# Packing the first chunk's attention scores into 15 steps, three of them shared by two pairs of head groups, and building the constant mask tile later

## The chip, the cores and the metric

The kernel runs on one core of a Trainium2 chip. The metric is the device time of one execution in microseconds (us). Of the kernel before, three timed runs gave 310.59, 310.47 and 310.94 us; their median is 310.59 us.

## What is computed

A transformer block on 2048 rows of 640 numbers: a layer norm, then sliding-window causal attention (32 heads of 20, each row sees itself and the 255 rows before it) and a gated unit, both on the normed input, both added to the input.

```python
xn = _layernorm(x)
qkv = (xn @ wqkv)                    # q, k, v: 32 heads of 20
scores = q @ k.T * 20 ** -0.5
mask = (i - j >= 0) & (i - j < 256)  # i: row of q, j: row of k
p = softmax(where(mask, scores, -1e9))
attn = (p @ v) @ wo
h = sigmoid(xn @ w_gate) * (xn @ w_up)
out = x + attn + h @ w_down
```

## The kernel before, in words

The 2048 rows are worked in four chunks (c = 0 to 3) of 512. Inside a chunk, the unit of attention is 64 rows (U = 64): a chunk has 8 units of queries, and its keys are its own 8 units and, from chunk 1 on, the last 4 of the chunk before. The 32 heads are 8 groups of 4; two groups form a **pair** (o = 0, 2, 4, 6), one on the upper and one on the lower 64 partitions of a score tile.

A **step** is one score tile: `scores` (L484) fills a 4-bank PSUM tile `ps` with up to 8 columns of units for each of 4 heads, ScalarE takes the exponential of it into a `pT` tile (L497), and masks follow. A step lists **pieces** (j, q, n, col): key unit j against n query units from q on, put at column col. A piece is 8 matmuls, 2 groups by 4 heads. A key unit meets at most 5 query units; the first of them needs the causal (diagonal) mask and the fifth the window's (old) mask. GpSimd makes these masks on `pT` by `affine_select` (L508), two instructions for a mask, one for each half of the partitions. In the last kind of step of the later chunks the two masks stand side by side, and VectorE does both by one minimum with a constant tile `edge` (L501). `edge` holds zeros and a huge number; `make_edge` (L239) builds it on GpSimd with one memset (L240) and four selects (L244).

In the first chunk no key lies before row 0, so a pair needs 30 columns of units. `FIRST` lays them out in 4 steps of 8, 8, 6 and 8, that is 16 steps for four pairs. A later chunk needs 5 steps a pair (`LATER`).

`pv` (L512) multiplies a pair's `pT` tiles by v into two PSUM accumulators `acc` (L524); `finish_group` and `scale_group` turn and divide the result on VectorE. `pv` takes the pieces in an order of its own: widest first, in rounds with narrow ones, four-wide ones last.

The order of the work is written by hand (manual schedule): each engine runs its instructions in the order in which the program issues them, and waits on semaphores. The main loop (from L723) goes through the list of all steps t. It issues a pair's `pv` when t is in `due`: in chunk 0 two steps after the pair's last step, in later chunks one. Then it issues the step's scores, and then **fill**: other matrix work (gate and up projections `gu`, the next chunk's q, k and v, the down and output projections `out`), pulled from a queue of generators in equal shares by cost (`credit`, `cuts`). A generator's unit is for instance five matmuls of 512 columns (`pg`, L415, or `pu`, L422). Normalising the next chunk is mixed into this fill (`g_norms`): VectorE statistics, `rstds` on GpSimd (L267, L268), `xn` on VectorE (L273).

Before the loop stand chunk 0's norm, v, q and k; `make_edge()` is called right behind `g_qk(0)`. GpSimd has nothing between its memsets at the start and the first step's masks, so its queue reaches `edge` at once.

Five `pT` tiles rotate. `ps` is a single tile.

Of the kernel before, what the change touches and what calls it, by code (L numbers as in the profile page):

```python
# [17 lines left out]
CW = 512  # L18
NCH = S // CW
SBC = CW // P  # L20
HG = 4
NG = H // HG
# [6 lines left out]
SCALE = DH ** -0.5  # L29
# [6 lines left out]
MIN = mybir.AluOpType.min  # L36
# [3 lines left out]
EXP = mybir.ActivationFunctionType.Exp  # L40
# [5 lines left out]
U = 64  # L46
# [13 lines left out]

FIRST = (
    dict(pieces=((0, 0, 5, 0), (5, 5, 3, 5)), diag=(0, 2), old=(4, 1), units=8),
    dict(pieces=((1, 1, 5, 0), (6, 6, 2, 5), (4, 7, 1, 7)), diag=(0, 2), old=(4, 1), units=8),
    dict(pieces=((2, 2, 5, 0), (7, 7, 1, 5)), diag=(0, 2), old=(4, 1), units=6),
    dict(pieces=((3, 3, 5, 0), (4, 4, 3, 5)), diag=(0, 2), old=(4, 1), units=8),
)
LATER = (
    dict(pieces=((2, 2, 5, 2), (-3, 0, 2, 0), (7, 7, 1, 7)), diag=(2, 2), old=(1, 2), units=8),  # L70
    dict(pieces=((3, 3, 5, 1), (6, 6, 2, 6), (-4, 0, 1, 0)), diag=(1, 2), old=(0, 2), units=8),
    dict(pieces=((0, 0, 5, 3), (-2, 0, 3, 0)), diag=(3, 1), old=(2, 2), units=8),
    dict(pieces=((1, 1, 5, 0), (5, 5, 3, 5)), diag=(0, 2), old=(4, 1), units=8),
    dict(pieces=((-1, 0, 4, 0), (4, 4, 4, 4)), late=3, units=8),
)
SPAN = 5


def steps_of(c):
    return [(o, step) for o in range(0, NG, 2) for step in (LATER if c else FIRST)]  # L80


def pieces_of(g):
# [10 lines left out]
def kernel(  # L94
# [11 lines left out]
    nc = tc.nc  # L106
# [4 lines left out]
    def pool(name, bufs, **kw):  # L111
        return ctx.enter_context(tc.tile_pool(name=name, bufs=bufs, **kw))
# [11 lines left out]
    op = pool("op", 7)  # L124
# [105 lines left out]
    for n in (6, 4):  # L230
        ps = ps_d.tile([P, CW], FP32, name="pwarm", tag="d")
# [179 lines left out]
    def g_gu(c, f0, f1):  # L411
        for f in range(f0, f1):
            pg = ps_d.tile([P, CW], FP32, name="pg", tag="d")
            for d in range(DC):
                nc.tensor.matmul(pg, lhsT=part(wg, d, f), rhs=xnT[c][:, d, :],  # L415
                                 start=(d == 0), stop=(d == DC - 1))
            th = tp.tile([P, CW], FP32, name="th")
            nc.scalar.activation(out=th, in_=pg, func=TANH, scale=0.5)  # L418
            yield 5 * MM
            pu = ps_d.tile([P, CW], FP32, name="pu", tag="d")  # L420
            for d in range(DC):
                nc.tensor.matmul(pu, lhsT=part(wu, d, f), rhs=xnT[c][:, d, :],  # L422
                                 start=(d == 0), stop=(d == DC - 1))
# [57 lines left out]
            yield 10 * 136  # L481


    def scores(c, o, step):  # L484
        pt = pp.tile([P, HG, PTW], BF16, name="pT")
        ps = ps_s.tile([P, HG, CW], FP32, name="ps")
        for j, q, n, col in step["pieces"]:
            kc, kb = divmod(c * CW // U + j, CW // U)
            for a in range(2):
                for i in range(HG):  # L490
                    nc.tensor.matmul(  # L491
                        ps[a * U:(a + 1) * U, i, col * U:(col + n) * U],
                        lhsT=qk["k", kc, o // GH][32 * i:32 * i + DH, o % GH + a, kb * U:(kb + 1) * U],
                        rhs=qk["q", c, o // GH][32 * i:32 * i + DH, o % GH + a, q * U:(q + n) * U],
                        start=True, stop=True)
        width = step["units"] * U
        nc.scalar.activation(out=pt[:, :, 0:width], in_=ps[:, :, 0:width], func=EXP, scale=SCALE)  # L497
        if "late" in step:
            u = step["late"]
            view = pt[:, :, u * U:(u + 2) * U]  # L500
            return pt, lambda: nc.vector.tensor_tensor(out=view, in0=view, in1=edge, op=MIN)  # L501

        for (u, n), base, sign in ((step["diag"], 0, 1), (step["old"], -1, -1)):
            for a in range(2):
                two = pt[a * U:(a + 1) * U].rearrange("p h (a b) -> p h a b", a=2)
                k, b = divmod(u, SPAN)
                view = two[:, :, k:k + n, b * U:(b + 1) * U]
                nc.gpsimd.affine_select(out=view, in_=view, pattern=[[0, HG], [0, n], [sign, U]],  # L508
                                        compare_op=GE, fill=0.0, base=base, channel_multiplier=-sign)
        return pt, None  # L510

    def pv(c, o, parts):  # L512
        accs = [ps_d.tile([P, CW], FP32, name="acc", tag="d") for _ in range(2)]

        flat = sorted(((pt, *piece) for step, pt in parts for piece in step["pieces"]), key=lambda x: -x[3])
        late = [x for x in flat if SPAN - 1 == x[3]]
        rounds = ([x for x in flat if x[3] == SPAN], [x for x in flat if x[3] < 3], [x for x in flat if x[3] == 3] + late)
        flat = [x for r in itertools.zip_longest(*rounds) for x in r if x]
        for k, (pt, j, q, n, col) in enumerate(flat):
            kb, u = divmod(c * CW // U + j, 2)  # L520
            for a, acc in enumerate(accs):
                for i in range(HG):
                    h = o // 2 * HG + i
                    nc.tensor.matmul(  # L524
                        acc[32 * i:32 * i + 32, q * U:(q + n) * U],
                        lhsT=vt[kb][a * U:(a + 1) * U, u, h * VW:h * VW + 32],
                        rhs=pt[a * U:(a + 1) * U, i, col * U:(col + n) * U],
                        start=(k == 0), stop=(k == len(flat) - 1), skip_group_check=True)
        for a, acc in enumerate(accs):
            finish_group(c, o + a, acc)  # L530
# [145 lines left out]
    for _ in g_qk(0):  # L676
        pass
    load_rest()
    make_edge()

    fill = Fill()
    GU = 10 * MM
# [3 lines left out]
    def later(load, *args):  # L686
        load(*args)
        yield 0
# [2 lines left out]
    norms2 = g_norms(2, True)  # L691
    norms3 = g_norms(3, False)
    fill.add("gu0a", mix(g_gu(0, 0, 4), norms1, 4, 1, False), 4 * GU)
    fill.add("gu0b", mix(g_gu(0, 4, 12), norms1, 0), 8 * GU)
    fill.add("x2", later(load_x, 2), 0)
    fill.add("wo_i", later(turn_wo), 0)
# [13 lines left out]
    fill.add("out2", g_out(2, (), g_gu(3, 0, 1)), OUT + GU)  # L710
    fill.add("gu3", g_gu(3, 1, 12), 11 * GU)

    todo = [(c, k, o, step) for c in range(NCH) for k, (o, step) in enumerate(steps_of(c))]
    ends = {(c, o): t for t, (c, _, o, _) in enumerate(todo)}
# [8 lines left out]
    for t, (c, k, o, step) in enumerate(todo):  # L723
# [11 lines left out]
        pt, late = scores(c, o, step)  # L735
        parts.setdefault((c, o), []).append((step, pt))
# [11 lines left out]
    c = NCH - 1  # L748
# [62 lines left out]
```

## Time and profile before

| | |
|---|---|
| median of three runs | 310.59 us (310.47 to 310.94) |
| the profiled execution's own time | 309.89 us |
| its span in the profile | 308.2 us |
| TensorE matmul busy | 300.2 us, 97% of the span |
| ScalarE, VectorE, GpSimd busy | 64%, 56%, 55% |
| exponentials, 128x2048 / 128x1536 | 1878 / 1446 ns each, 72 and 4 of them |
| score matmuls and pv matmuls | 1440 and 1440 |

How to read it: times are microseconds from the start of the span. In the timeline a line gives start, duration, engine, source line, operation, the tile written and those read, how many instructions were merged into the line, and in brackets how long the engine was idle before it and what released it. A merged line names only the form of its first instruction. PE is TensorE's matmul, DVE is VectorE, ACT is ScalarE, POOL is GpSimd. Matmuls overlap in the pipeline, so the duration of one is longer than the distance to the next start; the distances between starts are the cost. The 1.7 us between the span and the execution's own time lie outside of the program's instructions.

### The profile page before, as it was taken

To read this page: it belongs to the slowest core of one execution; us is meant where nothing else is said; L and a number is where in the kernel's file an instruction comes from. 1 tells how busy PE (TensorE), PEld (TensorE's weight loads), DVE (VectorE), ACT (ScalarE), POOL (GpSimd) and SP (SyncE) were. 2 spreads that over 40 slices of the span, in tenths; PEclk is the share of its full clock that TensorE was granted. 3 is DMA by queue.
4 is the path that set the end of the run, shared out by engine and by line. 5 is a ranking of instruction groups with operands and counts; after the bars stand their busy time and mean duration, and the time that the engine had idled before them with its cause. 6 is when DMAs were issued, how large, how long until landed. Compare 5 with 4: busy or idle time off the path is not lost.

```text
span 308.2 us, 9938 instructions
## 1 busy us (share of the span) xinstructions
PE 300.2 (97%) x4276; PEld 167.5 (54%) x4311; DVE 171.2 (56%) x339; ACT 198.4 (64%) x197; POOL 168.7 (55%) x308
## 2 busy tenths in 40 slices
PE   7999999999999999999999999999999999999995
PEld 3654444545657654554457664554546664444774
DVE  5633657648698364497946164383734536363523
ACT  6923777698854649888674647878585547687000
POOL 6000687687874828576682728557372937566000
PEclk9999999999999999999999999999999999999999
DMA  7997986984709253720015312660000200000202
GB/s 216 366 315 249 317 168 200 348 231 146 232 2 126 70 178 123 219 81 2 3 24 87 87 57 74 196 189 0 5 0 2 86 26 21 2 2 9 81 21 67
DMA packets 40461, 35.68 MB, mean 116 GB/s; under 512 B 10561, under 2 KB 39873, under 8 KB 40385
## 3 DMA queue, kind: packets, MB, share of 16 engines
q1 hardware_dynamic: 39552, 34.27, 38.4%
q8 instruction: 34, 0.56, 0.8%
q10 hardware_dynamic: 864, 0.77, 0.8%
q14 instruction: 11, 0.08, 0.1%
HBM read 23.63 MB, written 10.26 MB: 110 GB/s over the span
## 4 chain that ended last, share of the span: by engine, by line
PE 96%; issue 1%; DMA 1%; DVE 1%; ACT 0%; SPq 0%
PE y L436 18%; PE pu L422 17%; PE pg L415 17%; PE pqk L300 14%; PE ps L491 9%; PE pv L330 7%; PE y L443 7%; PE acc L524 6%; DMA xc<-in_A_x_dram 1%; PE pt L280 0%; ACT xn L621 0%; DVE xn L273 0%; DVE xn L632 0%; DVE stats L253 0%; SPq L157 0%
## 5 line engine op out<-in xcount | busy, mean ns | idle before, releaser
L508 POOL TENSOR_SCALAR_AFFINE_SELECT pT<-pT 64x512 bf16<-64x512 bf16 (+1 forms) x256 | 157.1, 614 | 109.3 <-ACT pT L497 97.0
L497 ACT ACTIVATE pT<-ps 128x2048 bf16<-128x2048 f32 (+1 forms) x76 | 141.0, 1855 | 59.8 <-PE ps L491 57.9
L426 DVE SCALAR_TENSOR_TENSOR h<-th,pu 128x512 bf16<-128x512 f32 x48 | 32.8, 683 | 51.4 <-PE pu L422 45.0
L422 PE MATMUL pu<-xnT,wu 128*128 128x512 bf16 x228 | 59.0, 380 | 0.7 <-issue 0.2
L415 PE MATMUL pg<-xnT,wg 128*128 128x512 bf16 x226 | 58.5, 380 | 1.0 <-issue 0.3
L436 PE MATMUL y<-wd,h 128*128 128x320 bf16 (+2 forms) x396 | 56.8, 295 | 0.0
L300 PE MATMUL pqk<-xnT,wqkv 128*128 128x512 bf16 x191 | 45.4, 381 | 0.6 <-issue 0.2
L436 PEld LDWEIGHTS <-h 128*128 128x128 bf16 x396 | 36.7, 98 | 15.9 <-issue 1.8
L418 ACT ACTIVATE th<-pg 128x512 f32<-128x512 f32 x48 | 28.6, 595 | 15.5 <-PE pg L415 15.4
L415 PEld LDWEIGHTS <-wg 128*128 128x128 bf16 x240 | 22.2, 98 | 25.8 <-issue 1.8
L422 PEld LDWEIGHTS <-wu 128*128 128x128 bf16 x240 | 22.0, 98 | 25.5 <-issue 2.0
L300 PEld LDWEIGHTS <-wqkv 128*128 128x128 bf16 x200 | 22.5, 119 | 18.9 <-issue 1.6
L536 DVE STREAM_TRANSPOSE t<-acc 128x512 f32<-128x512 f32 x32 | 21.1, 696 | 20.1 <-PE acc L524 20.1
L491 PE MATMUL ps<-qT,kT 20*64 20x320 bf16 (+4 forms) x1440 | 32.1, 260 | 0.0
L491 PEld LDWEIGHTS <-kT 20*64 20x64 bf16 x1440 | 15.4, 103 | 24.8 <-issue 21.4
L447 DVE SCALAR_TENSOR_TENSOR rows<-y,rows 128x320 bf16<-128x320 f32 x30 | 14.4, 487 | 25.9 <-PE y L443 25.8
L548 DVE TENSOR_TENSOR on<-t,rec 128x320 bf16<-128x320 f32 (+4 forms) x48 | 27.8, 579 | 1.1
L330 PE MATMUL pv<-wqkv,xnT 128*128 128x320 bf16 x160 | 26.0, 300 | 0.0
L443 PE MATMUL y<-wo,oc 128*128 128x320 bf16 (+2 forms) x165 | 24.2, 295 | 0.0
L339 DVE CAST v<-pv 64x320 bf16<-64x320 f32 x29 | 14.1, 487 | 12.6 <-PE pv L330 12.3
L524 PE MATMUL acc<-pT,v 64*32 64x320 bf16 (+4 forms) x1440 | 19.7, 253 | 0.0
L524 PEld LDWEIGHTS <-v 64*32 64x32 bf16 x1440 | 16.3, 91 | 5.7 <-ACT pT L497 1.7
(48 smaller groups left out, 156.7 us busy)
## 6 DMA issues: line engine op xcount, KB each, us to landing
qT<-sq SPq DMA_DIRECT2D x16, 256.0 KB
kT<-sk SPq DMA_DIRECT2D x16, 256.0 KB
sq<-st SPq DMA_DIRECT2D x20, 128.0 KB
sk<-st SPq DMA_DIRECT2D x20, 128.0 KB
out_dram<-rows SPq DMA_DIRECT2D x15, 160.0 KB
wg<-in_B_w_gate_dram SPq DMA_DIRECT2D x4, 480.0 KB
wu<-in_B_w_up_dram SPq DMA_DIRECT2D x4, 480.0 KB
xc<-in_A_x_dram SPq DMA_DIRECT2D x3, 640.0 KB
```

The source lines that it names most:

```text
L300: nc.tensor.matmul(ps, lhsT=wt[:, m, :], rhs=xnT[c][:, d, :], start=(d == 0), stop=(d == DC - 1))
L330: nc.tensor.matmul(ps[:, 0:HALF], lhsT=xnT[c][:, d, s * P:(s + 1) * P], rhs=wqkv[:, d, 2 * D + hf * HALF:2 * D + (hf + 1) * HALF], start=( ...
L415: nc.tensor.matmul(pg, lhsT=part(wg, d, f), rhs=xnT[c][:, d, :], start=(d == 0), stop=(d == DC - 1))
L418: nc.scalar.activation(out=th, in_=pg, func=TANH, scale=0.5)
L422: nc.tensor.matmul(pu, lhsT=part(wu, d, f), rhs=xnT[c][:, d, :], start=(d == 0), stop=(d == DC - 1))
L426: nc.vector.scalar_tensor_tensor(out=h, in0=th, scalar=1.0, in1=pu, op0=ADD, op1=MULT)
L436: nc.tensor.matmul(y[:, 0:cut[1] - cut[0]], lhsT=ht[c, f][:, s * P:(s + 1) * P], rhs=wd[:, f, cut[0]:cut[1]], start=(f == 0), stop=False)
L443: nc.tensor.matmul(y[:, 0:cut[1] - cut[0]], lhsT=oc[c, m][:, s * P:(s + 1) * P], rhs=wo[:, m, cut[0]:cut[1]], start=False, stop=(m == DC - 1))
L491: nc.tensor.matmul(ps[a * U:(a + 1) * U, i, col * U:(col + n) * U], lhsT=qk["k", kc, o // GH][32 * i:32 * i + DH, o % GH + a, kb * U:(kb + ...
L497: nc.scalar.activation(out=pt[:, :, 0:width], in_=ps[:, :, 0:width], func=EXP, scale=SCALE)
L508: nc.gpsimd.affine_select(out=view, in_=view, pattern=[[0, HG], [0, n], [sign, U]], compare_op=GE, fill=0.0, base=base, channel_multiplier ...
L524: nc.tensor.matmul(acc[32 * i:32 * i + 32, q * U:(q + n) * U], lhsT=vt[kb][a * U:(a + 1) * U, u, h * VW:h * VW + 32], rhs=pt[a * U:(a + 1) ...
```

## The change

Each pair of the first chunk now has three steps of its own, all of them full (8 columns). What is left of each pair, the five columns of key unit 3 and one of key unit 7, goes into three **shared** steps, one behind each of the pairs 0, 1 and 2: the first holds 6 columns of pair 0 and 2 of pair 1, the second 4 of pair 2 and 4 of pair 1, the third 6 of pair 3 and 2 of pair 2. Chunk 0 has 15 steps. In a shared step two neighbouring masks go to VectorE's minimum with `edge` (`late`), the others to GpSimd. `due` becomes one step after the pair's last step for the first three pairs of chunk 0 too; only the last pair of chunk 0 keeps two. `make_edge` moves from ahead of the loop into the fill queue, behind the first four gate/up blocks (`gu0a`).

```diff
 FIRST = (
-    dict(pieces=((0, 0, 5, 0), (5, 5, 3, 5)), diag=(0, 2), old=(4, 1), units=8),
-    dict(pieces=((1, 1, 5, 0), (6, 6, 2, 5), (4, 7, 1, 7)), diag=(0, 2), old=(4, 1), units=8),
-    dict(pieces=((2, 2, 5, 0), (7, 7, 1, 5)), diag=(0, 2), old=(4, 1), units=6),
-    dict(pieces=((3, 3, 5, 0), (4, 4, 3, 5)), diag=(0, 2), old=(4, 1), units=8),
+    dict(pieces=((0, 0, 5, 0), (5, 5, 3, 5)), masks=(DIAG2, OLD1)),
+    dict(pieces=((1, 1, 5, 0), (6, 6, 2, 5), (4, 7, 1, 7)), masks=(DIAG2, OLD1)),
+    dict(pieces=((2, 2, 5, 0), (4, 4, 3, 5)), masks=(DIAG2, OLD1)),
+)
+
+SHARED = (
+    dict(pairs=((0, ((3, 3, 5, 0), (7, 7, 1, 5))), (1, ((3, 3, 2, 6),))), masks=(DIAG1, (1, 6, 1)), late=4),
+    dict(pairs=((2, ((3, 3, 4, 0),)), (1, ((3, 5, 3, 4), (7, 7, 1, 7)))), masks=(DIAG1,), late=6),
+    dict(pairs=((3, ((3, 3, 5, 0), (7, 7, 1, 7))), (2, ((3, 7, 1, 5), (7, 7, 1, 6)))),
+         masks=(DIAG1, (1, 7, 1), OLD1), late=5),
 )
...
+    for p in range(NG // 2):
+        steps += [whole(p, step) for step in (LATER if c else FIRST)]
+        if c == 0 and p < len(SHARED):
+            pieces = [(2 * q, *piece) for q, made in SHARED[p]["pairs"] for piece in made]
+            steps.append(dict(SHARED[p], pieces=pieces))
+    return steps
...
-        for j, q, n, col in step["pieces"]:
+        for o, j, q, n, col in sorted(step["pieces"], key=lambda x: -x[3]):
...
-        width = step["units"] * U
-        nc.scalar.activation(out=pt[:, :, 0:width], in_=ps[:, :, 0:width], func=EXP, scale=SCALE)
+        nc.scalar.activation(out=pt[:, :, 0:CW], in_=ps, func=EXP, scale=SCALE)
+        for diag, u, n in step["masks"]:
+            base, sign = (0, 1) if diag else (-1, -1)
...
-    make_edge()
...
     fill.add("gu0a", mix(g_gu(0, 0, 4), norms1, 4, 1, False), 4 * GU)
+    fill.add("edge", later(make_edge), 0)
     fill.add("gu0b", mix(g_gu(0, 4, 12), norms1, 0), 8 * GU)
...
-    due = {t + (1 if n else 2): (n, o) for (n, o), t in ends.items()}
+    due = {t + (2 if (n, o) == (0, NG - 2) else 1): (n, o) for (n, o), t in ends.items()}
```

`DIAG1` and `DIAG2` are the diagonal mask at column 0, and at columns 0 and 5; `OLD1` is the old mask at column 4. A mask of two units is a pair of selects of 64x512 elements, of one unit a pair of 64x256. The masks of the later chunks are the same as before, in the new notation. `pv` now gets its pieces with the tile that holds each, since a pair's pieces may lie in another pair's step.

More of the change, by code (lines that the diff above doesn't have):

```diff
@@ L47 @@
 PTW = 10 * U
+SPAN = 5
+DIAG2, OLD2 = (1, 0, 2), (0, 4, 2)
+DIAG1, OLD1 = (1, 0, 1), (0, 4, 1)
 FIRST = (
[L64 to L67 removed]
+    dict(pieces=((0, 0, 5, 0), (5, 5, 3, 5)), masks=(DIAG2, OLD1)),
+    dict(pieces=((1, 1, 5, 0), (6, 6, 2, 5), (4, 7, 1, 7)), masks=(DIAG2, OLD1)),
+    dict(pieces=((2, 2, 5, 0), (4, 4, 3, 5)), masks=(DIAG2, OLD1)),
+)
@@ L68 @@
+SHARED = (
[3 more added lines that the diff above has]
+         masks=(DIAG1, (1, 7, 1), OLD1), late=5),
 )
 LATER = (
-    dict(pieces=((2, 2, 5, 2), (-3, 0, 2, 0), (7, 7, 1, 7)), diag=(2, 2), old=(1, 2), units=8),
-    dict(pieces=((3, 3, 5, 1), (6, 6, 2, 6), (-4, 0, 1, 0)), diag=(1, 2), old=(0, 2), units=8),
@@ L72 @@
-    dict(pieces=((0, 0, 5, 3), (-2, 0, 3, 0)), diag=(3, 1), old=(2, 2), units=8),
-    dict(pieces=((1, 1, 5, 0), (5, 5, 3, 5)), diag=(0, 2), old=(4, 1), units=8),
-    dict(pieces=((-1, 0, 4, 0), (4, 4, 4, 4)), late=3, units=8),
+    dict(pieces=((2, 2, 5, 2), (-3, 0, 2, 0), (7, 7, 1, 7)), masks=((1, 2, 2), (0, 1, 2))),
+    dict(pieces=((3, 3, 5, 1), (6, 6, 2, 6), (-4, 0, 1, 0)), masks=((1, 1, 2), (0, 0, 2))),
+    dict(pieces=((0, 0, 5, 3), (-2, 0, 3, 0)), masks=((1, 3, 1), (0, 2, 2))),
+    dict(pieces=((1, 1, 5, 0), (5, 5, 3, 5)), masks=(DIAG2, OLD1)),
@@ L75, with whole @@
+    dict(pieces=((-1, 0, 4, 0), (4, 4, 4, 4)), masks=(), late=3),
 )
-SPAN = 5
 def steps_of(c):
-    return [(o, step) for o in range(0, NG, 2) for step in (LATER if c else FIRST)]
+    def whole(p, step):
+        return dict(step, pieces=[(2 * p, *piece) for piece in step["pieces"]])
+    steps = []
+    for p in range(NG // 2):
[3 more added lines that the diff above has]
+            steps.append(dict(SHARED[p], pieces=pieces))
@@ L481, in g_out, with scores @@
             yield 10 * 136
-    def scores(c, o, step):
+    def scores(c, step):
         pt = pp.tile([P, HG, PTW], BF16, name="pT")
         ps = ps_s.tile([P, HG, CW], FP32, name="ps")
-        for j, q, n, col in step["pieces"]:
+        for o, j, q, n, col in sorted(step["pieces"], key=lambda x: -x[3]):
             kc, kb = divmod(c * CW // U + j, CW // U)
@@ L495, in scores @@
                         start=True, stop=True)
-        width = step["units"] * U
[L497 to L503, printed above, removed]
+        nc.scalar.activation(out=pt[:, :, 0:CW], in_=ps, func=EXP, scale=SCALE)
+        for diag, u, n in step["masks"]:
+            base, sign = (0, 1) if diag else (-1, -1)
             for a in range(2):
@@ L509, in scores @@
                                         compare_op=GE, fill=0.0, base=base, channel_multiplier=-sign)
-        return pt, None
+        if "late" not in step:
+            return pt, None
+        view = pt[:, :, step["late"] * U:(step["late"] + 2) * U]
+        return pt, lambda: nc.vector.tensor_tensor(out=view, in0=view, in1=edge, op=MIN)
     def pv(c, o, parts):
         accs = [ps_d.tile([P, CW], FP32, name="acc", tag="d") for _ in range(2)]
-        flat = sorted(((pt, *piece) for step, pt in parts for piece in step["pieces"]), key=lambda x: -x[3])
-        late = [x for x in flat if SPAN - 1 == x[3]]
+        flat = sorted(parts, key=lambda x: -x[3])
+        late = [x for x in flat if x[3] == SPAN - 1]
         rounds = ([x for x in flat if x[3] == SPAN], [x for x in flat if x[3] < 3], [x for x in flat if x[3] == 3] + late)
@@ L711 @@
     fill.add("gu3", g_gu(3, 1, 12), 11 * GU)
-    todo = [(c, k, o, step) for c in range(NCH) for k, (o, step) in enumerate(steps_of(c))]
-    ends = {(c, o): t for t, (c, _, o, _) in enumerate(todo)}
-    due = {t + (1 if n else 2): (n, o) for (n, o), t in ends.items()}
+    todo = [(c, k, step) for c in range(NCH) for k, step in enumerate(steps_of(c))]
+    ends = {(c, piece[0]): t for t, (c, _, step) in enumerate(todo) for piece in step["pieces"]}
+    due = {t + (2 if (n, o) == (0, NG - 2) else 1): (n, o) for (n, o), t in ends.items()}
     cuts = [(ends[n, NG - 2] + 2 + n, f"out{n}") for n in range(NCH - 1)] + [(len(todo), None)]
@@ L722 @@
     fill.shut = {"out0", "out1", "out2"}
-    for t, (c, k, o, step) in enumerate(todo):
+    for t, (c, k, step) in enumerate(todo):
         if k == 0 and c > 0:
@@ L734 @@
                 fill.shut.discard(f"out{pair[0]}")
-        pt, late = scores(c, o, step)
-        parts.setdefault((c, o), []).append((step, pt))
+        pt, late = scores(c, step)
+        for o, *piece in step["pieces"]:
+            parts.setdefault((c, o), []).append((pt, *piece))
         last, label = next(x for x in cuts if t < x[0])
```

## The prediction

> **What bounds the kernel now.** I read the page's busy shares and its chain of work first, then the timelines of TensorE and GpSimd over the first chunk's steps, and the forms of the mask instructions.
>
> ```profile
> PE 300.2 (97%) x4276; PEld 167.5 (54%) x4311; DVE 171.2 (56%) x339; ACT 198.4 (64%) x197; POOL 168.7 (55%) x308
> PE 96%; issue 1%; DMA 1%; DVE 1%; ACT 0%; SPq 0%
> ```
>
> TensorE is on the chain for 96% of the span, so each microsecond put into its queue, as work or as a wait, lengthens the run by itself. A step, from the timeline of TensorE:
>
> ```profile
> 39.64 0.42 PE L491 MATMUL ps<-qT,kT 20*64 20x320 bf16 x16
> 39.99 1.25 PE L422 MATMUL pu<-xnT,wu 128*128 128x512 bf16 x5
> 41.08 1.24 PE L415 MATMUL pg<-xnT,wg 128*128 128x512 bf16 x5
> 42.25 0.42 PE L491 MATMUL ps<-qT,kT 20*64 20x320 bf16 x16
> 44.87 1.04 PE L524 MATMUL acc<-pT,v 64*32 64x320 bf16 x72
> 45.84 0.43 PE L491 MATMUL ps<-qT,kT 20*64 20x320 bf16 x24
> ```
>
> Read the distances between starts: scores 0.35, `pu` 1.09, `pg` 1.17, then the next scores. There is no room between them; TensorE waits for nobody here. The whole `pv` takes 0.97 (44.87 to 45.84). The masks of the same stretch, on GpSimd:
>
> ```profile
> 33.19 2.40 POOL L508 TENSOR_SCALAR_AFFINE_SELECT pT<-pT 64x512 bf16<-64x512 bf16 x4 [27.47 <-ACT pT L497]
> 35.68 0.23 POOL L267 TENSOR_SCALAR rstds<-mvs 128x4 f32<-128x4 f32 x1
> 35.99 1.04 POOL L268 TENSOR_TENSOR rstds<-rstds,neghalf 128x4 f32<-128x4 f32 x1
> 37.00 5.02 POOL L508 TENSOR_SCALAR_AFFINE_SELECT pT<-pT 64x512 bf16<-64x512 bf16 x8
> 42.17 4.00 POOL L508 TENSOR_SCALAR_AFFINE_SELECT pT<-pT 64x512 bf16<-64x512 bf16 x6 [0.15 <-ACT pT L497]
> ```
>
> One step's four selects take 2.4 to 2.5. From 33.19 on GpSimd has no idle time to speak of: it is 55% busy over the span but full here. Step 3's masks, the first four of the last line, end near 44.7, and the first `pv` starts at 44.87. The page's average hides that this stage has almost no slack on GpSimd, although `pv` stands two steps behind the pair's last scores.
>
> **The step that goes.** All score columns stay: 4 pairs of 30 units before, 15 full tiles of 8 now, 120 each. In `pv` also. What goes is a step's fixed cost. Eight units cost 0.35 to 0.36 (42.25 to 42.61), six cost 0.30 (37.07 to 37.37): 0.026 a unit, 0.21 for eight, so about 0.14 is fixed. A block of five 512-column matmuls takes 1.08 in a row (26.34 to 27.42) and 1.17 ahead of scores, 0.09 more; behind scores 1.09, 0.01 more. Sum: **-0.25**. Two more pieces (38 for 36) cost no column, and matmuls by themselves nothing: a step's 24 in three pieces take 0.36 (45.84 to 46.20) as 16 in two do. ScalarE loses four exponentials of 1446 ns and gains three of 1878: it waits for scores in this stage, so nothing. The fill is the same work in 15 shares.
>
> **The mask tile.** In the old place `edge` is hidden: memset from 3.18, four selects to 5.72, while GpSimd has nothing else until 33.19. So 2.54 is its length, gaps included. In the order of the changed program, GpSimd's queue has it behind step 0's masks and `rstds`, ahead of step 1's. It starts at 37.00 and all masks behind it move by 2.54. It issues no DMA, and SyncE's queue has its DMAs in the same order as before.
>
> **The first `pv`.** It now stands one step earlier, before step 4's scores. Step by step:
> - TensorE: step 3's scores start at 39.64 + 0.05 (step 2 has two units more) = 39.69. Then 0.36 for them, and three blocks of fill in the new order, 1.09 + 1.08 + 1.17: `pv` is reached at 43.39 and would end at 44.36.
> - GpSimd: `edge` 37.00 to 39.54, step 1's and 2's masks 5.02 and a gap, 44.61. Of the shared step the first `pv` needs the diagonal mask, two selects of 458 ns with gaps: 45.64.
> - `pv` takes the wide piece of the shared step last. Its second half waits to 45.64 + 0.06 (a released engine starts that much later, as POOL behind ACT at 33.19). Four matmuls and the switch, about 0.2: scores start at 45.90.
>
> That is **+1.54** against 44.36. Everything on TensorE is queued behind this wait. VectorE's minimum is not late: the exponential ends near 42.2 and the minimum takes 0.43.
>
> Without the move of `edge` the mask would end at 43.10, before its piece is due at 44.2: no wait. With it and the old distance of two steps there would be none either.
>
> **A second place.** The fill shifts against the steps in later chunks. I compared each `pv` with the masks that it needs; most have the room that other pairs have before. One has not, chunk 1's first pair. Its fourth step's masks stand behind `rstds`, which waits for VectorE's statistics, not for TensorE:
>
> ```profile
> 91.52 0.23 POOL L267 TENSOR_SCALAR rstds<-mvs 128x4 f32<-128x4 f32 x1 [0.55 <-DVE mvs L259]
> 91.83 1.05 POOL L268 TENSOR_TENSOR rstds<-rstds,neghalf 128x4 f32<-128x4 f32 x1
> 92.85 2.50 POOL L508 TENSOR_SCALAR_AFFINE_SELECT pT<-pT 64x512 bf16<-64x512 bf16 x4
> 95.56 1.29 PE L524 MATMUL acc<-pT,v 64*32 64x320 bf16 x96
> ```
>
> The masks end at 95.35. The last piece that needs them comes 0.83 into `pv`: 96.39, a margin of 1.0. In the new order ten 320-column matmuls (0.136 each, by the chain's 12 in 1.63) fewer stand between the `pv` before and this one, while VectorE's work stays where it was. So 1.36 - 1.04 = **+0.3**.
>
> The second and third `pv` have no wait by the same sums. After the first wait TensorE is late and GpSimd's backlog is gone; the shared steps' parts that they need are VectorE's alone. The tightest is VectorE's minimum of the third shared step, 0.2 to 0.4 ahead of its piece; if it is late, a few tenths.
>
> **A rule against the change.** VectorE's minimum has two inputs in SBUF, and now runs beside selects.
>
> ```profile
> L501 DVE TENSOR_TENSOR pT<-pT,edge x12: 424/426/427, 94.6 to 284.4; 128x512 bf16<-128x512 bf16 x12
> 94.60 0.43 DVE L501 TENSOR_TENSOR pT<-pT,edge 128x512 bf16<-128x512 bf16 x1 [0.18 <-ACT pT L497]
> ```
>
> All twelve take the same time, also this one, whose stretch lies inside GpSimd's 92.85 to 95.35. The Trainium skill, "SBUF — State Buffer", section "SBUF: two separate sides", says that such an instruction and a GpSimd one that reads SBUF exclude each other for a whole instruction. By it the first shared step's minimum could hold up the masks by 0.43, and the sum would be +2.0; by the row it is +1.6. I go by the row.
>
> **The start.** With `edge` gone from 3.18 to 5.72, VectorE's `xn` (L273) at 4.83, which took 0.61 beside its selects, may take 0.45 as its like (L632) does at 5.97. TensorE's first transposes wait for it. But the second ones wait for L632, which follows ScalarE's root; that ends near 5.73 in any case, 0.03 ahead of the reciprocal at 5.77. Between 0 and -0.17; I take 0.
>
> **Sum.** -0.25 + 1.54 + 0.3 = **+1.6 us**. Against the profiled execution, 309.89 (span 308.2 and 1.7 around it), that is 311.5. The median of the runs shown, 310.59, lies 0.7 above that execution, within what runs differ by (310.47 to 310.94); I put the change on the median: **312.2 us**, 0.5% slower. What a measurement can tell from no change is about 0.2%, 0.6 us.
>
> Bounds of the unknown term, the first wait: if the select that meets VectorE's `xn` in the stretch from 37.0 on (two xn passes of up to 0.79) is held up twice more, and the piece waits for all four selects of its step, not two, 1.03 more, it is 2.6. From below, if the second `pv` half needed only the first of the two selects, 0.52 less, 1.0. I keep 1.54, since each select's length has a row.
>
> **Rivals.**
> - *More waits.* A minimum behind VectorE's queue in the second or third shared step, or the upper bound above: each +0.3 to +1.0, together 312.6 to 313.3. For it: margins of 0.2 to 0.4. Against: the rows' equal lengths. 0.15.
> - *Only a small wait.* Should TensorE's own order be later than I count, or the mask of the shared step be early, +0.2 to +0.6 remains: 310.8 to 311.2. 0.13.
> - *Faster.* GpSimd isn't late at all: this decides at one point, whether the shared diagonal mask ends before 44.2. It needs 1.45 less on GpSimd between 37.0 and 45.6, as if `edge` fell into idle time. Then the removed step is left, -0.25, and with the start's 0.17 and the lack of the second wait 310.1 to 310.4, which can't be told from no change. The full row of selects from 33.19 speaks against it. 0.10.
> - *The forecast*, both waits, 311.4 to 312.6: 0.62.
>
> Range: 310.6 to 313.2 leaves out the faster rival and what lies beyond the upper one. Faster by over 0.2% needs a gain that no row shows: 0.05. Within 0.2% (309.97 to 311.21): the small wait and most of the faster rival, 0.17. Slower: 0.78.
>
> **What would show it.** In the changed profile: `edge` on GpSimd between 37 and 39.6; GpSimd without a gap to 46; the first `pv` taking about 2.5 in place of 0.97, ended by GpSimd; step 4's scores near 45.9 (step 4 before: 42.25); a wait of a few tenths in chunk 1's first `pv`; 15 exponentials of 128x2048 in chunk 0, and fifteen minima in all. I'm wrong if the first `pv` runs through in 1 us, if `edge` stands ahead of step 0's masks, or if TensorE's loss appears in a stage I have not named.

## The result: 2.35 us slower, and the profile after

| | before | after |
|---|---|---|
| median | 310.61 us (309.91 to 310.94, 6 runs) | 312.96 us (312.41 to 313.65, 6 runs) |
| ratio | 1 | 1.0069, 95% interval 1.0052 to 1.0085 |
| profiled execution, its span | 309.89, 308.2 us | 312.41, 310.6 us |

The direction is as forecast, and 312.96 lies inside the range given; the size is 2.35 in place of 1.6. It lies above the 311.4 to 312.6 that the prediction gave as the forecast, and among the times of its rival "more waits". The profiled execution of after is the fastest of its six (312.41). The page's line of busy times, which in the forecast opened the argument, now reads:

```profile
PE 301.6 (97%) x4308; PEld 168.5 (54%) x4343; DVE 172.9 (56%) x342; ACT 198.5 (64%) x196; POOL 165.2 (53%) x304
```

It shows nothing of the loss: TensorE's busy time also holds matmuls that are drawn out by waits, and the shares are within two points of the old ones. The place is found in GpSimd's timeline of the first steps:

```profile
33.47 2.40 POOL L522 TENSOR_SCALAR_AFFINE_SELECT pT<-pT 64x512 bf16<-64x512 bf16 x4 [30.04 <-ACT pT L515]
35.95 0.23 POOL L286 TENSOR_SCALAR rstds<-mvs 128x4 f32<-128x4 f32 x1
36.27 1.04 POOL L287 TENSOR_TENSOR rstds<-rstds,neghalf 128x4 f32<-128x4 f32 x1
37.27 0.53 POOL L259 MEMSET edge<- 128x512 bf16 x1
37.87 1.79 POOL L263 TENSOR_SCALAR_AFFINE_SELECT edge<-edge 64x256 bf16<-64x256 bf16 x4
39.72 7.08 POOL L522 TENSOR_SCALAR_AFFINE_SELECT pT<-pT 64x512 bf16<-64x512 bf16 x12
```

`edge` (L259, L263) has slid between `rstds` and the next masks, with no gap on either side. TensorE's timeline of the same stretch:

```profile
42.49 1.24 PE L441 MATMUL pu<-xnT,wu 128*128 128x512 bf16 x5
43.67 0.90 PE L541 MATMUL acc<-pT,v 64*32 64x320 bf16 x52
44.77 0.35 PE L541 MATMUL acc<-pT,v 64*32 64x320 bf16 x12 [0.21 <-POOL pT L522]
45.30 0.32 PE L541 MATMUL acc<-pT,v 64*32 64x320 bf16 x4 [0.17 <-POOL pT L522]
45.82 0.32 PE L541 MATMUL acc<-pT,v 64*32 64x320 bf16 x4 [0.21 <-POOL pT L522]
46.07 0.42 PE L510 MATMUL ps<-qT,kT 20*64 20x320 bf16 x16
```

The first `pv` takes 2.40 (43.67 to 46.07), where it took 0.97, and GpSimd ends each of its waits. The brackets add up to only 0.59, because a bracket begins only where the matmul before it ends by the record, and without a wait the next one starts well before that; the distance between starts shows the loss, 1.43.

The fifth `pv`, chunk 1's first, and the masks that it needs, from the timelines of GpSimd and TensorE in after:

```profile
94.37 2.50 POOL L522 TENSOR_SCALAR_AFFINE_SELECT pT<-pT 64x512 bf16<-64x512 bf16 x4
95.72 1.66 PE L541 MATMUL acc<-pT,v 64*32 64x320 bf16 x96
```

The masks end at 96.87, 1.15 into the `pv`; the forecast put the last piece that needs them 0.83 into it. The two executions, piece by piece, by distances between starts on TensorE (after less before):

| place | us |
|---|---|
| start of the first scores (31.03 for 30.75) | +0.28 |
| first `pv` | +1.43 |
| third `pv` (1.04 for 0.97), second `pv` (0.95) | +0.05 |
| the rest of chunk 0 up to chunk 1's first scores | -0.24 |
| fifth `pv`, chunk 1's first pair (1.59 for 1.22) | +0.37 |
| `y` waits for an h, at 157.53 | +0.36 |
| scores at 170.36 wait for ScalarE's exponential of the step before | +0.13 |
| scores at 206.33 take 0.93 for 0.36 | +0.57 |
| from the last `pv` to the end (19.75 for 20.28) | -0.53 |

The sum is +2.42; the spans differ by 2.4. The last row is the final store: TensorE's last matmul ends 3.1 us ahead of the span's end, before 3.6. I don't know why. It goes with the layout: the eleven kernels with 15 steps have 3.09 to 3.29 there, the three with 16 steps 3.54 to 3.63.

So the forecast's three terms (-0.24, +1.43, +0.37) make 1.56. The rest lies in places that it didn't name: +1.06 at 157.53, 170.36 and 206.33, less 0.25 at the start and the end together.

### The profile page after: what moved, and what is told of

Same layout as the page of the kernel before. It is cut to its first block, busy times and chain, and to the rows that moved or that the text cites. A ratio compares the mean times of both kernels' runs of the same rounds, so it can differ in the third digit from the quotient of the medians.

```text
span 310.6 us, 10001 instructions
## 1 busy us (share of the span) xinstructions
PE 301.6 (97%) x4308; PEld 168.5 (54%) x4343; DVE 172.9 (56%) x342; ACT 198.5 (64%) x196; POOL 165.2 (53%) x304
## 4 chain that ended last, share of the span: by engine, by line
PE 82%; DVE 5%; POOL 5%; DMA 3%; issue 2%; ACT 1%; SPq 0%; ACTq 0%; DVEq 0%; POOLq 0%
PE y L455 14%; PE pqk L319 14%; PE pu L441 13%; PE pg L434 13%; PE pv L349 7%; PE ps L510 7%; PE y L462 6%; PE acc L541 6%; POOL pT L522 3%; DMA xc<-in_A_x_dram 2%; DMA wqkv<-in_A_wqkv_dram 2%; ACT pT L515 1%; DVE on L565 1%; DVE stats L272 1%; DVE oc L569 1%
## 5 line engine op out<-in xcount | busy, mean ns | idle before, releaser
L522 POOL TENSOR_SCALAR_AFFINE_SELECT pT<-pT 64x512 bf16<-64x512 bf16 (+1 forms) x252 | 153.6, 609 | 115.0 <-ACT pT L515 103.1
L515 ACT ACTIVATE pT<-ps 128x2048 bf16<-128x2048 f32 x75 | 140.8, 1877 | 61.8 <-PE ps L510 59.6
L541 PE MATMUL acc<-pT,v 64*32 64x320 bf16 (+4 forms) x1456 | 20.9, 252 | 0.7 <-POOL pT L522 0.6
```

The lines of the kernel that those rows point to most:

```text
L515: nc.scalar.activation(out=pt[:, :, 0:CW], in_=ps, func=EXP, scale=SCALE)
L541: nc.tensor.matmul(acc[32 * i:32 * i + 32, q * U:(q + n) * U], lhsT=vt[kb][a * U:(a + 1) * U, u, h * VW:h * VW + 32], rhs=pt[a * U:(a + 1) ...
```

## The experiments

My theory: `edge` on a full GpSimd makes the first wait, and the fifth `pv`'s wait is that of masks behind `rstds`. The rivals: the earlier `pv` by itself, or a time that is given back at a later wait whichever one is taken away. All kernels start from the changed one, except two that start from the one before. Names that come up: `h` is the gated product, `th` the tanh in it, `y` the sum of the down and output projections. From chunk 1 on, q and k go through `st` buffers to memory (`sq`, `sk`) and are loaded from there as `qT` and `kT`; `xnT` is `xn` transposed by a DMA, `xc` the rows of x, `wo_i` and `wd` weights. Each kernel is compared with runs of the kernel before made beside it, whose medians lie between 310.39 and 310.64. The numbers by kernel (durations of `pv` and waits of TensorE of 0.2 or more, each from that kernel's profiled execution, us; the pause is the distance between the starts of two matmuls):

| kernel | ratio to before, 95% interval | 1st pv | 3rd pv | wait for kT, 78 | 5th pv | wait for xnT, 109 | y for h, 156 | pause in scores, 206 |
|---|---|---|---|---|---|---|---|---|
| before | 1 | 0.97 | 0.97 | 0 | 1.22 | 0 | 0 | 0 |
| after | 1.0052 to 1.0085 | 2.40 | 1.04 | 0 | 1.59 | 0 | 0.36 | 0.57 |
| e1: edge early | 1.0031 to 1.0071 | 1.01 | 1.51 | 0 | 1.60 | 0 | 0.36 | 0.82 |
| e2: before, edge late | 1.0040 to 1.0072 | 2.57 | 0.97 | 0 | 1.22 | 0 | 0 | 0 |
| e3: first pv later | 1.0043 to 1.0094 | 0.97 | 1.82 | 0 | 1.59 | 0 | 0.84 | 0.29 |
| e4: e1, statistics later | 1.0031 to 1.0081 | 1.01 | 2.19 | 0 | 1.22 | 0 | 0.84 | 0.56 |
| e5: e4, nine st | 1.0061 to 1.0112 | 1.00 | 0.97 | 1.04 | 1.22 | 1.29 | 0.84 | 0.33 |
| e7: e4, code shifted | 1.0053 to 1.0081 | 0.97 | 1.63 | 1.37 | 1.22 | 0.88 | 0.36 | 0 |
| e8: e4, last xn later | 1.0004 to 1.0047 | 1.01 | 2.22 | 0 | 1.22 | 1.14 | 0 | 1.07 |
| e9: e5, e7, e8 together | 1.0033 to 1.0070 | 0.99 | 0.97 | 1.71 | 1.22 | 0.51 | 0 | 0 |
| e10: e1, first xn earlier | 1.0029 to 1.0061 | 0.97 | 0.97 | 0 | 1.59 | 0 | 0.84 | 0.72 |
| e11: e10 and two repairs | 1.0016 to 1.0049 | 0.97 | 0.97 | 1.39 | 1.22 | 0 | 0 | 0.89 |
| e12: before, first xn earlier | 0.9982 to 1.0021 | 0.97 | 0.97 | 0 | 1.22 | 0 | 0.75 | 0 |
| e13: e11, code shifted | 0.9984 to 1.0020 | 0.98 | 0.97 | 1.30 | 1.22 | 0 | 0 | 0 |

The table is read across: wherever a wait is gone, look to its right. A profile is one execution; waits for DMA above all differ between executions, so that e8's and e11's profiled executions were among the slowest of their runs (313.12 with a median of 311.14; 313.22 with 311.78), and e10's and e1's were the fastest (311.26 with 312.05; 311.50 with 312.21). The verdicts go by the ratios.

### e1: the mask tile back ahead of the loop

```diff
+    make_edge()
     fill = Fill()
...
-    fill.add("edge", later(make_edge), 0)
```

> The changed kernel with make_edge() back ahead of the loop, all else as changed. Theory A (the mask tile on GpSimd, 2.4 us, makes the first pv's wait): the first pv takes 0.97 us in place of 2.40, chunk 1's first pv still takes about 1.6, and the time is 1.4 us below the changed kernel's 312.96, about 311.5, so 0.8 to 1.1 above before. Theory B (the pv that comes one step earlier is the cause, whatever the tile does): the first pv still waits over 1 us and the time stays within 0.4 of 312.96. Theory C (the loss lies in the later chunks, where the fill is shifted): the first pv becomes short but the kernel stays over 2 us slower than before.

The first `pv`'s wait is gone (1.01), and so the cause of that wait is right. The time is not: 312.21, 1.8 above before, between what theory A (0.8 to 1.1) and theory C (over 2) expected. The third `pv` now waits for VectorE's minimum:

```profile
68.61 0.85 PE L541 MATMUL acc<-pT,v 64*32 64x320 bf16 x56
69.83 0.36 PE L541 MATMUL acc<-pT,v 64*32 64x64 bf16 x24 [0.37 <-DVE pT L527]
```

### e2: the kernel before, with nothing but the mask tile late

```diff
-    make_edge()
...
+    fill.add("edge", later(make_edge), 0)
```

> The kernel before with nothing changed but the place of make_edge: in the fill, behind gu0a, as the changed kernel has it. The first pv keeps its two steps. Theory A: step 3's masks end near 47.1 in place of 44.7, the first pv, reached at 44.87, takes about 2.5 us in place of 0.97, and the time is 1.4 to 1.6 us above before, near 312.1. Theory B: with two steps between the last scores and the pv there is no wait, pv 1.0, time as before within 0.2.

The first `pv` takes 2.57, though it stands two steps behind its scores here. The move of `edge` alone costs 1.6 of `pv` time and 0.4 to 0.7% of the run; the new steps aren't needed for it. This is theory A, in the time too (312.06). The waits, from TensorE's timeline of e2:

```profile
46.76 0.83 PE L524 MATMUL acc<-pT,v 64*32 64x192 bf16 x24 [0.47 <-POOL pT L508]
47.80 0.32 PE L524 MATMUL acc<-pT,v 64*32 64x320 bf16 x4 [0.21 <-POOL pT L508]
```

In the old layout the last step of the pair has four selects of its own on GpSimd, and its last mask ends at 47.75 here. A step more of distance doesn't save that.

### e3: the first pv two steps behind, as before

```diff
-    due = {t + (2 if (n, o) == (0, NG - 2) else 1): (n, o) for (n, o), t in ends.items()}
+    due = {t + (2 if (n, o) in ((0, 0), (0, NG - 2)) else 1): (n, o) for (n, o), t in ends.items()}
```

> The changed kernel with the first pair's pv two steps behind its last scores in place of one; the mask tile stays in the fill. Theory A and B agree that the first pv's wait goes: 1.0 us in place of 2.40, and the time is 1.4 below 312.96, near 311.5. Were the wait made by GpSimd's whole load of masks in chunk 0, a later pv (the second) would wait in its place. If C holds, the time stays over 2 us above before in spite of it.

This too takes the first wait away (0.97): the masks that it needs end at 46.00, and it starts at 46.52. So in the new layout the wait takes both, the late `edge` and the shorter distance. The time stays, 312.93 for 312.96, as theory C has it. The third `pv` grows to 1.82, and `y` to 0.84. Time given back, twice over.

### e4: e1, and the third chunk's statistics later

```diff
-    fill.add("out0", mix(g_out(0, g_gu(1, 2, 3)), norms2, 1, 1), OUT + GU)
+    fill.add("out0", mix(g_out(0, g_gu(1, 2, 3)), norms2, 4, 1), OUT + GU)
```

> As e1 (mask tile ahead of the loop), and the norm of chunk 2 begins three units of fill later in chunk 1, so that GpSimd's rstds stands behind the fourth step's masks and not ahead of them. Theory A with the second place of the prediction: chunk 1's first pv takes 1.22 in place of 1.59, and the time is 0.3 to 0.4 below e1's. All waits found are gone then and the step removed is left: 0.0 to 0.3 below before, near 310.4. Theory C: further waits in the later chunks keep it 0.5 or more above before.

The fifth `pv` falls to 1.22, as the theory of `rstds` says; the third takes 2.19 and the time is 312.09, not the 310.4 of theory A; theory C holds. Nothing that e4 changes against e1 stands ahead of the third `pv`, so that 2.19 for 1.51 is a difference between executions. What holds the third `pv`? ScalarE's timeline ahead of it, in e4:

```profile
64.54 0.58 ACT L325 CAST st<-pqk 128x512 bf16<-128x512 f32 x1
66.77 1.07 ACT L325 CAST st<-pqk 128x512 bf16<-128x512 f32 x2 [1.65 <-DMA sq<-st]
67.73 1.90 ACT L515 ACTIVATE pT<-ps 128x2048 bf16<-128x2048 f32 x1
```

The exponential at 67.73, whose minimum the third `pv` needs, is queued behind casts of chunk 1's k, and the first of these waits for a free `st` buffer, that is for a DMA. The two-step distance of before hid this.

### e5: e4 with nine st buffers

```diff
-    stp = pool("stp", 6)
+    stp = pool("stp", 9)
```

> The stretch with the edge tile early and the second chunk's statistics later (the run before this one, span 310.2), with nine st buffers where there were six. Theory (the third pv waits for a minimum whose exponential stands on ScalarE behind st casts that wait for a free st buffer, 'ACT L325 CAST st<-pqk [1.65 <-DMA sq<-st]'): that cast's wait goes below 0.3, the third pv falls from 2.19 to 1.0 to 1.3 us, the time falls by 0.7 to 1.1. Rival 1 (the minimum is late for another reason: the port, or the exponential's own scores): third pv stays above 1.9 and the time within 0.3. Rival 2 (given back again): third pv falls, but the wait of y for h at about 156 us, 0.84 there, or a later one grows by as much and the time moves by under 0.3.

In e5 the same casts and exponential stand like this:

```profile
66.30 0.58 ACT L325 CAST st<-pqk 128x512 bf16<-128x512 f32 x1 [0.41 <-PE pqk L319]
66.81 1.88 ACT L515 ACTIVATE pT<-ps 128x2048 bf16<-128x2048 f32 x1
```

No wait for a DMA, and the third `pv` is 0.97: the buffers were it. But the run is no faster, 313.15. ("The second chunk's statistics" in this and a later expectation are those of chunk 2, which e4 moves.) TensorE now waits 1.04 at chunk 1's first scores for `kT` and 1.29 for `xnT`: the second rival, at two new places. The second is of my making: e4's later statistics issue chunk 2's transposes at 100.8 and on in place of 93.8.

### e7: e4 with TensorE's code shifted

```diff
+    ps = ps_d.tile([P, CW], FP32, name="pwarm", tag="d")
+    for k in range(24):
+        nc.tensor.matmul(ps[:, 0:2], lhsT=ones[:, 0:P], rhs=ones[:, 0:2], start=(k == 0), stop=(k == 23))
     for n in (6, 4):
```

> Edge early and statistics later, with 24 matmuls of two columns added to the warm-up, which shift every later TensorE instruction by 48 places in the program. The pause of 0.24 to 0.50 us inside the scores at about 206 us stands in four kernels at the same instruction, has no semaphore in the program, and ends 2.3 to 2.4 us after the start of a transfer of queue q8 (kind 'instruction') of 16 KB. Theory (TensorE's code arrives late there): the pause leaves that instruction, and either is gone or stands 48 instructions earlier, among v or pg matmuls that are slower than scores, so that it is under 0.15; time lower by 0.2 to 0.4, the added matmuls costing 0 to 0.3 at the start. Rival (something tied to that step, such as its operands): 0.2 us or more remain at the fourth score matmul of that step.

The pause in after's scores, from TensorE's timeline:

```profile
206.33 0.33 PE L510 MATMUL ps<-qT,kT 20*64 20x320 bf16 x3
206.91 0.33 PE L510 MATMUL ps<-qT,kT 20*64 20x320 bf16 x8 [0.26 <-issue]
```

Three matmuls, then nothing until 206.91, and no releaser. The same steps in e7:

```profile
206.29 1.24 PE L437 MATMUL pg<-xnT,wg 128*128 128x512 bf16 x5
207.47 0.43 PE L513 MATMUL ps<-qT,kT 20*64 20x320 bf16 x24
```

The pause is gone with a shift of 48 instructions and no other edit. It stands in all eight 15-step kernels without the shift and in none of the three with it. In the eight it ends 2.26 to 2.57 us after the start of a 16 KB transfer of kind "instruction". The length of the pause varies from 0.29 to 1.07, and the distance to that transfer hardly does. So the pause depends on the count of instructions ahead of it, and not on the step's operands; that it is code that comes late is the reading that fits both, though no view names whose code the transfer brings. The time isn't lower as expected (312.46): here too `kT` is waited for.

### e8: e4 with the fourth chunk's xn later

```diff
-    fill.add("gu1b", mix(g_gu(1, 7, 12), norms3, 0, 1, False), 5 * GU)
-    fill.add("out1", mix(g_out(1, g_gu(2, 0, 1)), itertools.chain(norms3, g_turns(3)), 1, 3), OUT + GU)
+    fill.add("gu1b", mix(g_gu(1, 7, 12), itertools.islice(norms3, 7), 0, 1, False), 5 * GU)
+    fill.add("out1", mix(g_out(1, g_gu(2, 0, 1)), itertools.chain(norms3, g_turns(3)), 1, 2), OUT + GU)
```

> Edge early and statistics later, with the fourth chunk's normalisation (four VectorE operations xn) put wholly behind the first y matmuls instead of three of the four ahead of them, and its statistics left where they were. Theory (y at about 156 us waits for an h that is queued on VectorE behind two xn operations): the wait of y, 0.84 there, falls below 0.15 and the time by 0.5 to 0.9. Rival (the h is late for its own matmuls or its tanh): the wait stays above 0.4, time within 0.2. Rival 2: the wait moves to the next product that needs VectorE, time within 0.3.

`y`'s wait is gone, and it stays gone in the later kernels that have this edit (e9, e11, e13): 311.14, ratio 1.0004 to 1.0047, the best so far. The interval overlaps that of e4 (1.0031 to 1.0081), so how much of the gain is this wait's stays open.

### e9: e4 with all three

> The new score steps with all four repairs: edge tile early, second chunk's statistics later, nine st buffers, the fourth chunk's normalisation later, TensorE's code shifted by 48. Theory (the change's fewer step is worth 0.25 us and all the loss is waits of these four kinds): no pv above 1.3, no y or score wait above 0.2, time 310.0 to 310.6, that is 0 to 0.4 below the kernel before. Rival 1 (the 15-step order has a cost of its own, beside the waits): all waits gone and still 0.4 or more slower than before. Rival 2 (a wait removed comes back as another): some wait of 0.4 or more at a place that none of the runs so far shows, time 311 to 312.

It has the edits of e5, e7 and e8 together, and takes 311.69, not 310.0 to 310.6. Every wait known until then is gone from chunk 0 and at 156 and 206. What is left, from the view of TensorE's waits:

```profile
PE ps L513 <- DMA kT<-sk: 1.7, 1, 1.7
PE pqk L322 <- DMA xnT<-xn: 0.5, 1, 0.5
```

Columns: total, times, longest. Chunk 1's first scores wait for the keys. Close behind TensorE stands a second bound, SyncE's queue of DMAs: transposes of `xnT`, then `xc`, `wo_i`, `wd`, then chunk 1's q and k out to memory and back. How near it stands: in e7, e9 and e13, which wait for it, the scores start 2.7 to 2.8 after the issue of `kT`; in before they start 3.3 after it (75.17 to 78.45) and don't wait. By these loads the slack was some 0.5. It isn't the same in every execution: in e5 and e11 the scores waited too, and started 3.5 and 4.5 after the issue.

### e10: e1 with the second chunk's first xn earlier

Where does that queue lose time? Its start in before and in e1, from SyncE's timeline:

```profile
39.81 5.27 SPq L284 DMA_TRANSPOSE xnT<-xn  x4
45.13 0.58 SPq L140 DMA_DIRECT2D xc<-in_A_x_dram  x1
```

```profile
39.92 5.80 SPq L303 DMA_TRANSPOSE xnT<-xn  x4
45.77 0.96 SPq L159 DMA_DIRECT2D xc<-in_A_x_dram  x1
```

And VectorE's timeline in e1, from which the third transpose gets its input:

```profile
42.25 0.42 DVE L527 TENSOR_TENSOR pT<-pT,edge 128x512 bf16<-128x512 bf16 x1
42.59 1.11 DVE L292 TENSOR_SCALAR xn<-xc,mvs,rstds 128x640 bf16<-128x640 bf16 x2
```

The first shared step's minimum, new in chunk 0, stands between the second `xn` and the third. The third transpose is issued 1.87 behind the second (1.31 before), and everything in the queue moves.

```diff
-    fill.add("gu0a", mix(g_gu(0, 0, 4), norms1, 4, 1, False), 4 * GU)
+    fill.add("gu0a", mix(g_gu(0, 0, 4), norms1, 2, 1, False), 4 * GU)
```

> The changed kernel with the edge tile early and the second chunk's first normalisation (statistics and xn) started two half-parts of gate/up earlier, so that all four xn stand ahead of the first shared step's minimum on VectorE. In the run with the edge tile early alone (312.21, span 309.7) that minimum stood between the second and the third xn: the third transposing DMA was issued 1.87 us after the second where the kernel before has 1.31, and SyncE's whole chain of issues after it came later, wo_i at 46.79 for 45.77, the first sq<-st at 58.89 for 58.08. Theory (that chain sets when chunk 1's st buffers come free and when its kT lands, so that TensorE cannot use the time that the other repairs give it): transposes back to back, wo_i at 45.8 or earlier, the casts on ScalarE ahead of the third shared exponential wait less than 0.3, the third pv 1.0 instead of 1.51, first scores of the second chunk at 78.1 to 78.5 for 78.82, time 311.3 to 311.9. Rival 1 (the chain is set by the bytes, not by its start): first sq<-st stays at 58.5 or later and the third pv above 1.3, time within 0.2 of 312.2. Rival 2 (earlier statistics hurt the first h or the weights' loads): TensorE waits of 0.3 or more before 45 us, time the same or more.

The first `sq<-st` is issued at 56.88 (e1 58.89), the third `pv` takes 0.97 with six `st` buffers, and chunk 1's first scores start at 78.22, earlier than in before (78.45). These are the theory's waits. The time moved less, 312.05 for e1's 312.21 (ratios 1.0045 and 1.0051, with intervals that overlap): the fifth `pv`, `y` and the pause are left.

### e11, e12 and e13: the rest, and a control

e11 is e10 with e8's edit and `norms2, 2, 1`. e13 is e11 with e7's shift. e12 is the kernel before with e10's edit alone.

> The same with two more repairs, smaller than those that overshot before: the third chunk's statistics one part later (three before, which made its transposes late and TensorE wait 0.5 to 1.3 for xnT at about 109 us), and the fourth chunk's xn all behind the first y matmuls. Theory: pv of the second chunk's first pair 1.22, no wait for xnT above 0.2, y no wait, and what may be left is TensorE's code pause of 0.2 to 0.8 in the scores at about 206; time 310.2 to 311.0. If the fewer step is worth 0.25 and nothing is left but the code pause, the span is 308.2 - 0.25 + pause. Rival (a wait comes back again at the next place): one wait of 0.4 or more at a place other than 206, time above 311.2.

> The kernel before with only the second chunk's normalisation two half-parts earlier, as a control. Theory (the kernel before has no wait for chunk 1's st buffers or kT, so that an earlier chain of issues gives it nothing): within 0.2 of before, 310.4 to 310.8, all pv at 0.97 and 1.22. Rival (the earlier normalisation is worth something by itself, and a gain seen in the changed kernel is not the change's): 0.3 or more below before.

> The run with three repairs and the edge tile early, and TensorE's code shifted by 48 instructions (24 warm-up matmuls of two columns). Theory (what the run with the repairs still loses is the code pause in the scores at about 206, 0.57 in its profile, and a kT that lands late by chance): no pause over 0.1 at 206, all pv at 0.97 and 1.22, no y wait, so a span of 308.0 to 308.4 from a start of the scores at 30.8, and a median of 310.4 to 311.0. Rival 1 (TensorE's code transfer now falls on the last sk<-st transfer, as it did in both earlier runs with the shift, where kT was issued 4.1 us after it and not 2.2): the first scores of the second chunk wait 0.8 or more for kT and the time stays at 311.3 to 311.9. Rival 2: the pause at 206 is only moved, 0.2 or more elsewhere without a named releaser.

e11: 311.78, where the theory had 310.2 to 311.0. No `pv` or `y` waits in it; the pause is left, and a wait for `kT` of 1.39, which is the rival's; the profiled execution also started its scores 1.5 late, at 32.30. e12: 310.78, the same as before. The kernel before gains nothing from an earlier queue, and in its profiled execution `y` waits for an h too, 0.75: that wait doesn't need the new steps. The other repairs were not tried on the kernel before; its profile shows no wait at the places that they mend. e13: 310.92, ratio 0.9984 to 1.0020. With five edits around it, the new layout neither costs nor brings anything that a measurement can tell. The pause is gone and the median as expected, but the span is 309.0 and not 308.0 to 308.4, because of a wait of the length that the first rival names:

```profile
77.08 1.24 PE L437 MATMUL pg<-xnT,wg 128*128 128x512 bf16 x4
79.63 0.43 PE L513 MATMUL ps<-qT,kT 20*64 20x320 bf16 x24 [1.30 <-DMA kT<-sk]
```

In the three kernels with shifted code (e7, e9, e13), `kT` is issued 3.9 to 4.3 us after the last `sk<-st`; in the eleven others 2.1 to 2.3. In these three a code transfer of 1.4 to 1.6 us lies at 74.1 to 74.6, between the two; in the others none starts between them. That speaks for the code transfer delaying the `sk<-st` that `kT` waits for, but I haven't tested it by itself. Less 1.30, e13's span of 309.0 would be 307.7, 0.5 under before, of which 0.35 is the shorter end that I can't explain (3.28 for 3.63); an estimate, and no kernel here reached it.

## Why the prediction was nearly right, point by point

- **The step removed, -0.25.** Right (its three parts make 0.24). From the start of the scores to chunk 1's first scores, less the waits above, it is 47.70 before (78.45 - 30.75) and 47.46 in after (79.97 - 31.03 - 1.48) and in e10 (78.22 - 30.78).
- **The first `pv`, +1.54.** Right: +1.43, at 43.67 as forecast (43.39, with a start 0.28 later), ended by GpSimd. `edge` took 2.39 of its 2.54. e1 takes the wait away, e2 makes it in the old layout.
- **The remark on the old distance** ("there would be none either") is right: e3, with `edge` late, has 0.97.
- **The fifth `pv`, +0.3.** Right: +0.37, and 1.22 once the statistics come later (e4).
- **The second and third `pv`: no wait.** Right in after (0.95, 1.04) by luck: TensorE was already late. The margin was too thin. "If it is late, a few tenths": it was 0.54 to 1.22 as soon as the first wait was gone (e1, e3, e4). e5 and e10 show why: the forecast had nothing on the queue of the minimum's exponential, behind casts that wait for `st` buffers.
- **"It issues no DMA, and SyncE's queue has its DMAs in the same order as before."** True and not enough. The order stayed; the time didn't, since the minimum stands ahead of the third `xn`.
- **"Most have the room."** I had compared `pv` with masks, and not `y` with h. The wait at 157.53 (+0.36) is missing from the sum; e12 shows such a wait without the new steps, and why it comes in one fill and not in another stays open.
- **The pause in the scores, +0.57.** Not seen, and not to be seen in the trace of before, which has no such pause.
- **The rule against the change.** I went by the row, twelve minima of 424 to 427 ns. The trace of after gives the Trainium skill's page "SBUF — State Buffer", section "SBUF: two separate sides", right that the two exclude each other:

```profile
L527 DVE TENSOR_TENSOR pT<-pT,edge x15: 424/426/727, 42.5 to 287.4; 128x512 bf16<-128x512 bf16 x15
42.54 0.61 DVE L527 TENSOR_TENSOR pT<-pT,edge 128x512 bf16<-128x512 bf16 x1 [0.17 <-ACT pT L515]
95.30 0.73 DVE L527 TENSOR_TENSOR pT<-pT,edge 128x512 bf16<-128x512 bf16 x1
```

  Smallest, median, largest: the largest is now 727 ns. The three minima that begin during a select, at 42.5, 70.3 and 95.3, take 0.61 to 0.73. Each of the three ends 0.26 to 0.27 after the recorded end of that select. So does the row of before that I leaned on, at 94.60, which began 0.16 ahead of a select's end: 0.16 and 0.27 make its 0.43, and there was no wait left to see. It works the other way too: the select that starts 0.04 behind the minimum at 57.51 takes 0.71, where others of its size take 0.45 to 0.46. In the first `pv`'s masks, however, the effect was not the 0.43: the select behind the minimum at 42.54 took 0.73 for 0.66, and GpSimd released the `pv` at about 45.8, against a forecast of 45.64.
- **The start: 0.** +0.28 in this execution. The starts of the fourteen profiled executions lie between 30.75 and 32.30 with both layouts, so this is no part of the change.
- **"Or if TensorE's loss appears in a stage I have not named."** By this sign of its own the prediction was wrong in part: 1.06 of the loss, at 157.53, 170.36 and 206.33, lies in stages that it had not named. The rival "more waits" had such a time, but by late minima and held-up masks, of which after shows less than 0.1.

In one sentence: each term that was worked out was right to 0.11, and the sum was short by what stands in no term.

## What to carry to other kernels

Before moving an instruction off an idle stretch, read the engine's timeline where it will land, not its share of the span: GpSimd was at 55% and full there. When a wait is removed and the time stays, look at the next waits to the right: in this kernel a DMA queue stood about half a microsecond behind TensorE, and much of what a repair brought was given back there. e9, which mends the other waits and leaves the start of that queue alone, is at a ratio of 1.0051; e13, where the queue starts earlier, is at 1.0002. It isn't the queue alone: e8, with the queue as it was, came nearer to before (1.0025) than e10 and e11 (1.0045, 1.0033). An added small instruction can cost through whoever queues behind it: a 0.42 us minimum moved a chain of DMAs by 0.6 (e1).

## What the runs showed of the hardware

- **A pause that goes with the place in the program.** A pause of 0.29 to 1.07 us without a releaser inside 24 short matmuls, at the same instruction in eight kernels. It goes when 24 matmuls of two columns are put ahead of it in the program. The Trainium skill, "Runtime: NRT & Kernel Launch", section "Instruction fetch mechanics", says that code is refilled in 16 KiB blocks of 256 instructions and that the cost of crossing into the next is mostly hidden. The trace agrees on the size of the transfers, 16 KB, and mostly on the rest: of the 34 such transfers in after, this is the only one near which TensorE stands idle for over 0.2 us without a releaser. That the pause is such a cost is likely, and shown only by the shift and by the steady distance of 2.26 to 2.57.
- **VectorE beside GpSimd.** In after, `xn` takes 0.40 to 0.45 us when no select runs, and beside selects 0.57 to 0.90 (0.43 once, begun 0.02 ahead of a select's end). The minimum takes 0.61 to 0.73 in place of 0.43 when it begins well inside a select, and a select that begins just behind a minimum 0.71 in place of 0.46.
